# The first MLP's w_in by seven products for its last 1024 tokens, with the attention ahead of it ordered by batches

## The chip, the cores and the metric

The kernel runs on one core of one Trainium2 chip. The metric is device time in microseconds, the median over runs. A profiled execution gives a trace: what each engine did, when, and what ended each wait. TensorE is PE in its rows (its weight loads are PEld), VectorE is DVE, ScalarE is ACT, SyncE, which issues most loads, is SP.

## The reference

Linear attention with a norm, then two MLPs on its 4608 tokens:

```python
kv = np.einsum('bhsd,bhse->bhde', k, v)            # batch 8, heads 8, seq 576, head_dim 64
out = np.einsum('bhsd,bhde->bhse', q, kv)
rms = np.sqrt(np.mean(out * out, axis=-1, keepdims=True) + 1e-06)
x = (out / rms * g_norm).transpose(0, 2, 1, 3).reshape(4608, 512)
h = x @ moe_w_in                                   # 512 x 2048
x = (h * (1.0 / (1.0 + np.exp(-h)))) @ moe_w_out   # 2048 x 512
h = x @ moe2_w_in
r = np.maximum(h, 0.0)
return (s * (r * r) + b) @ moe2_w_out
```

## The kernel before

A product of two fp32 matrices is made of three fp32r matmul passes: each operand is split into a rounded high part and the rest (`xh` and `xl`, `wh` and `wl`; a "split" is a cast on ScalarE and a difference on VectorE), and high x high, high x low and low x high are summed in PSUM. A matmul takes a 128x128 weight tile and up to 512 tokens.

The kernel has four stages, one for each weight matrix. Stages 2 to 4 (`Output`, `Hidden`) use seven products: rows and columns are halved, and four half products by eight become seven products of sums of quarters (P1 to P7), the sums of the weights being made ahead and kept in DRAM (`wd`). Stage 1 is plain: nine blocks j of 512 tokens, each 16 groups m of 12 matmuls (`emit_h`, L469 to L501), whose PSUM tile `ph` ScalarE turns by Silu into g; g goes to DRAM (`gt`), from where stage 2 loads it.

The program's order is written by hand: one loop over (j, m) emits a group, then what `first_stage` (L926) puts behind it. Each engine runs its instructions in the order in which they are written. Beside block j stands the attention of tokens 512(j+1) to 512(j+2), four tiles t of 128 tokens, which may lie across two batches (`load_next` and `emit_next`, L544 to L572): keys times values at m = 2 (`emit_kv`, tile `pkv`), the transpose of q from m = 3 on (`emit_qT`, `pq`), q times kv at m = 4 to 7 (`out_tile`, `po`, whose squares go to a sum and whose copy goes to the page `xnp`), the root by some small VectorE steps, the scaling of `xnp` at m = 10 and 11, and the transposes of x at m = 11 to 14 (`xT_tile`, `px`), from which ScalarE makes `xh` and VectorE `xl` of the next block. The PSUM tiles `pkv`, `pq`, `po` and `px` take turns in two buffers (tag `a`), `ph` in two others.

`do_some(steps, n)` runs n steps of the weight preparation of stages 2 and 3: a step is one part of the decoding of raw weights (`rebias` on ScalarE, `low`, `sign`, `merge` on VectorE, L149), of their sums, or one split whose result goes to `wd`. `defer(1, f)` issues a store one group later. `room(tag, ...)` is a named place in SBUF, and who writes it waits for all who used it before.

Of the kernel before, what the change touches and what calls it, by code (L numbers as in the profile page):

```python
# [17 lines left out]
def kernel(  # L18
# [36 lines left out]
    nc = tc.nc  # L55
# [55 lines left out]
    def token_runs(t0, n):  # L111
        done = 0
        while done < n:
            b, s = divmod(t0 + done, S)
            step = min(n - done, S - s)
            yield done, step, b, s
            done += step

# [47 lines left out]
    hi_t = {}  # L166

    def decode_first(i, *steps):
        for step in steps:
            if step == "high":  # L170
                h = hi_t[i] = room(f"W{12 + 2 * i}", [P, WN], F32R, f"wh{i}")
                nc.scalar.copy(h, wf_t[1, i])
            elif step == "rest":
                l = room(f"W{13 + 2 * i}", [P, WN], F32R, f"wl{i}")
# [184 lines left out]
    def load_q(t):  # L359
        a = q_pages[t % TT // 2][:, t % 2].rearrange("p (h d) -> p h d", h=H)  # L360
        for off, n, b, s in token_runs(t * P, P):
            nc.sync.dma_start(a[off:off + n], q[b, :, s:s + n, :].rearrange("h p d -> p h d"))
        q_t[t] = a

    def emit_qT(t):
        a = q_t.pop(t).rearrange("p h d -> p (h d)")
        ps = ps_a.tile([P, T], F32, tag="a", name=f"pq{t}")
        for p in range(NP):
            nc.tensor.transpose(ps[:, p * P:(p + 1) * P], a[:, p * P:(p + 1) * P], ident)  # L369
        qT = at_kvw[:, 0].rearrange("p (a t) -> p a t", a=NP)  # L370
        nc.scalar.copy(qT.rearrange("p a t -> p (a t)"), ps)
        qT_t[t] = qT

    def emit_out(t, ps, pairs):

        po = ps.rearrange("p h d -> p (h d)")
        for p in pairs:
            for off, n, b, s in token_runs(t * P, P):
                nc.tensor.matmul(  # L379
                    po[off:off + n, p * P:(p + 1) * P], qT_t[t][:, p, off:off + n], kvw[b % 2][:, p, :],  # L380
                    start=True, stop=True,
                )

    def emit_squares(t, ps, ms):

        sq = work.tile([P, H, D], F32, tag="sg", name=f"sq{t}", bufs=3)
# [3 lines left out]
    def rsqrt_steps(r):  # L390

        ms, h, y, a = (r[:, i, :] for i in range(4))
# [21 lines left out]
    def xn_page(t):  # L414
        return xn_pages[t % TT // 2][:, t % 2].rearrange("p (h d) -> p h d", h=H)
# [9 lines left out]
    def out_tile(t):  # L425
        j, i = divmod(t, TT)
        if i == 0:
            r_t[j] = small.tile([P, 4, TT * H], F32, tag="r", name=f"r{j}", bufs=1)
        ps = ps_a.tile([P, H, D], F32, tag="a", name=f"po{t}")
        emit_out(t, ps, range(NP))  # L430
        emit_squares(t, ps, r_t[j][:, 0, i * H:(i + 1) * H])
# [3 lines left out]
    def norm_tile(t):  # L435
        j, i = divmod(t, TT)
        emit_norm(t, xn_t[t], r_t[j][:, 2, i * H:(i + 1) * H])
# [5 lines left out]

    def emit_xT(t, ps):
        xn = xn_t.pop(t).rearrange("p h d -> p (h d)")
        for p in range(NP):
            nc.tensor.transpose(ps[:, p, :], xn[:, p * P:(p + 1) * P], ident)  # L447
        j, i = divmod(t, TT)
        xh, xl = x_tiles(j)
        c = slice(i * P, (i + 1) * P)  # L450
        nc.scalar.activation(xh[:, :, c], ps, AF.Identity, scale=gcol)  # L451
        nc.vector.scalar_tensor_tensor(xl[:, :, c], ps, gcol, xh[:, :, c], op0=ALU.mult, op1=ALU.subtract)

    def xT_tile(t):
        emit_xT(t, ps_a.tile([P, NP, P], F32, tag="a", name=f"px{t}"))
# [13 lines left out]
    def emit_h(j, m):  # L469
# [8 lines left out]
        if j < NB - 2:  # L478

            i = m % 2  # L480
            if i == 0:
                g_t[0] = room(f"W{4 + m // 2 % NA}", [P, 2, T], F32, f"g{j}_{m}")
            both = g_t[0]
            g, rows = both[:, i], slice(m - 1, m + 1)
        else:
            i = 1
            tag = f"W{m}" if j == NB - 2 and m < 3 * NA else ("gh_0", "gh_1", "gl_0", "gl_1")[m % 4]
            g = room(tag, [P, T], F32, f"g{j}_{m}")
        nc.scalar.activation(g, ps, AF.Silu)  # L489
        run_late()  # L490
        if i == 0:
            return
        if j == 0:
            to = gt[1][0][rows].rearrange("i h p t -> p (i h) t")
            defer(1, lambda: nc.scalar.dma_start(to, both.rearrange("p i (h t) -> p (i h) t", h=2)))
        elif j < NB - 2:
            to = gt[1][(j + 1) // 2][rows, (j + 1) % 2].rearrange("i p t -> p i t")
            defer(1, lambda: nc.scalar.dma_start(to, both))
        else:
            to = gt[1][(j + 1) // 2][m, (j + 1) % 2]  # L500
            defer(1, lambda: nc.scalar.dma_start(to, g))  # L501
# [25 lines left out]
    def first_qT(t, qs):  # L527
# [10 lines left out]
        qT_t[t] = qT.rearrange("p (a t) -> p a t", a=NP)  # L538
# [3 lines left out]
    XT0 = 2 * TT + 3  # L542

    def load_next(j, m):  # L544

        t0 = TT * (j + 1)
        if m < TT:
            load_q(t0 + m)
        if 4 <= m < 4 + NP and j + 2 < B:
            load_kv(j + 2, m - 4)  # L550

    def emit_next(j, m):

        t0 = TT * (j + 1)
        if m == 2 and j + 1 < B:
            emit_kv(j + 1, range(NP))
        i = m - NP
        if 0 <= i < TT:
            out_tile(t0 + i)
        if -1 <= i < TT - 1:  # L560
            emit_qT(t0 + i + 1)
        if i == TT - 1:
            between.extend(rsqrt_steps(r_t[j + 1]))
        if j > 0 and 0 <= i - TT + 1 < 3:
            run_between(4)
        if m in (XT0 - 1, XT0):
            run_between(len(between))
            i = 2 * (m - XT0 + 1)
            norm_tile(t0 + i)
            norm_tile(t0 + i + 1)  # L570
        if XT0 <= m < XT0 + 4:
            xT_tile(t0 + m - XT0)  # L572

# [8 lines left out]
    class Hidden:  # L582
# [5 lines left out]
        def __init__(self, stage):  # L588
            self.grid, self.gt = grid[stage], gt[stage]
# [3 lines left out]

        def load(self, b, o):

            opening = b == order[0]
            tag = {self.B11: "Q", self.B12: "XA", self.B22: "XB", self.B21: "K" if opening else "Q"}[o]
            h, c = int(o in (self.B12, self.B22)), 2 * int(o in (self.B21, self.B22))
            x = self.raw[b, o] = pair(tag, f"xs{b}_{o}")[:, :, :size[b]]
            nc.sync.dma_start(x, yt[b][c:c + 2, h].rearrange("c p t -> p c t"))  # L600

        def combine(self, b, o):
# [5 lines left out]
            elif o == self.T2:  # L608
                to = pair("wf_0", f"xt2_{b}")[:, :, :size[b]] if b == order[0] else self.raw[b, self.T1]
# [6 lines left out]
        def split(self, b, k):  # L616
# [11 lines left out]
            self.slots[b, k] = [[t[:, c] for c in range(2)] for t in (hi, lo)]  # L628
            nc.scalar.copy(hi, src)
            nc.vector.tensor_sub(lo, src, hi)  # L630

        def before(self, k, a):

            b = order[0]
# [11 lines left out]
        def behind(self, b, i, k):  # L646

            nb = self.next_of.get(b)
            if i == 0 and b == order[0] and k in (P5, P6, P2):
# [21 lines left out]
        def product(self, g, k):  # L671
# [5 lines left out]
            a = self.grid.tiles[k, i // 2][:, i % 2].rearrange("p s (c f) -> p s c f", c=2)  # L677
            x = self.slots[b, k]
            for n, (s, t) in enumerate(PASSES):
                for c in range(2):  # L680
                    nc.tensor.matmul(  # L681
                        ps, a[:, s, c], x[t][c], start=(k in (P1, P5) and n == c == 0),
# [6 lines left out]
        def out(self, g, f, h, slots):  # L689
            b = self.seq[g][0]  # L690
            self.turn += 1
            r = room(self.G_ROOMS[self.turn % (4 if b else 7)], [P, T], F32, f"g{b}_{f}_{h}")[:, :size[b]]
# [3 lines left out]
        def square(self, g, f, h, ps):  # L696
            r = self.out(g, f, h, 2)
# [3 lines left out]
        def add_square(self, g, f, h, x, y):  # L701
# [5 lines left out]
            nc.vector.scalar_tensor_tensor(r, r, 0.0, r, op0=ALU.max, op1=ALU.mult)  # L707
# [32 lines left out]
    class Output:  # L740
# [96 lines left out]
        def rows_out(self, b, h, r):  # L837
# [6 lines left out]
            if b == 0:  # L844
                rows = out[:T].rearrange("(p c) d -> c p d", c=TT)[2 * h + r]
            else:
                rows = out[(2 * b - 1 + h) * T + r * P:][:P]
            defer(1, lambda: nc.scalar.dma_start(rows, o))
# [75 lines left out]
    out2, hidden3, out4 = Output(2), Hidden(3), Output(4)  # L924

    def first_stage(j, m, steps):  # L926

        if j + 1 < NB:
            load_next(j, m)
# [12 lines left out]
        if j + 1 < NB:  # L942
            emit_next(j, m)
        if j > 0:
            do_some(steps, 3 if m >= 12 else 2)
        elif m == MT - 1:
            do_some(steps, 1)
        if j == NB - 2 and m >= 4:
            grid[2].load()
        if j == NB - 1:  # L950
            if m < 4:
                out2.load(m + 1)
            else:
                out2.load(m - 7)
            if m >= 2:
                grid[2].load()
            if m in (10, 12):
                out2.make(m // 2 - 4)
# [33 lines left out]
    with tc.manual_schedule():  # L992
# [26 lines left out]
        r = r_t[0] = small.tile([P, 4, TT * H], F32, tag="r", name="r0", bufs=1)  # L1019
# [7 lines left out]
        for t in range(TT):  # L1027
            emit_out(t, pss[t], (0, 1))
# [3 lines left out]
        for p in (2, 3):  # L1032
            first_kv(p)
            for t in range(TT):
                emit_out(t, pss[t], (p,))
            load_kv(1, p)
        for t in range(TT):
            emit_squares(t, pss[t], r[:, 0, t * H:(t + 1) * H])
        decode_first(1, "high")
        warm_up(4)  # L1040
        for step in rsqrt_steps(r):
            step()
        for t in range(TT):
            emit_norm(t, pss[t], r[:, 2, t * H:(t + 1) * H])
        for t in range(TT):
            if t < 2:
                xT_tile(t)
            else:
                emit_xT(t, ps_y.tile([P, NP, P], F32, tag=f"y{t - 2}", name=f"px{t}"))
# [22 lines left out]
        for j in range(NB):  # L1072
# [3 lines left out]
        do_some(steps, 1000)  # L1076
# [37 lines left out]
```

## Time and profile before

| what | value |
|---|---|
| median of 3 runs | 1576.95 us (1576.92 to 1578.34) |
| the profiled execution | 1576.17 us |
| its span, from the first to the last instruction | 1574.4 us |
| TensorE busy | 1554.8 us, 99% of the span |
| VectorE, ScalarE busy | 959.1 us (61%), 802.7 us (51%) |
| mean DMA rate over the span | 222 GB/s |

Matmuls are pipelined and their ends are modelled, so the time of one matmul is read from start to start of a row and the next, not from its own duration. An engine's wait is named by what ended it. Durations in rows are in us unless marked ns.

### The profile page before, as it was taken

To read this page: it belongs to the slowest core of one execution; us is meant where nothing else is said; L and a number is where in the kernel's file an instruction comes from. 1 tells how busy PE (TensorE), PEld (TensorE's weight loads), DVE (VectorE), ACT (ScalarE), POOL (GpSimd) and SP (SyncE) were. 2 spreads that over 40 slices of the span, in tenths; PEclk is the share of its full clock that TensorE was granted. 3 is DMA by queue.
4 is the path that set the end of the run, shared out by engine and by line. 5 is a ranking of instruction groups with operands and counts; after the bars stand their busy time and mean duration, and the time that the engine had idled before them with its cause. 6 is when DMAs were issued, how large, how long until landed. Compare 5 with 4: busy or idle time off the path is not lost.

```text
span 1574.4 us, 21756 instructions
## 1 busy us (share of the span) xinstructions
PE 1554.8 (99%) x8232; PEld 1307.6 (83%) x8232; DVE 959.1 (61%) x1298; ACT 802.7 (51%) x1268; POOL 1.6 (0%) x8
## 2 busy tenths in 40 slices
PE   7999999999999999999999999999999999999998
PEld 5888888888888888888889788888889888888888
DVE  4736544654420958586857676767655858585745
ACT  3644554555432444444445565656555454555455
POOL 0000000000000000000000000000000000000000
PEclk9999999999999999999999999999999999999999
DMA  8978998796779663636259956574566982626251
GB/s 254 276 222 280 292 290 267 270 309 222 234 254 325 222 216 106 232 100 236 88 169 345 352 201 232 193 260 168 214 230 253 349 285 94 228 83 229 89 160 55
DMA packets 225609, 349.58 MB, mean 222 GB/s; under 512 B 56544, under 2 KB 94432, under 8 KB 225504
## 3 DMA queue, kind: packets, MB, share of 16 engines
q1 hardware_dynamic: 160064, 238.85, 46.3%
q10 hardware_dynamic: 65440, 109.34, 18.6%
q8 instruction: 65, 1.06, 0.3%
q14 instruction: 40, 0.33, 0.1%
HBM read 209.72 MB, written 138.41 MB: 221 GB/s over the span
## 4 chain that ended last, share of the span: by engine, by line
PE 93%; DMA 4%; DVE 1%; ACT 1%; issue 0%; SPq 0%; ACTq 0%; DVEq 0%
PE ph L475 25%; PE qy L891 18%; PE qv L891 12%; PE qx L891 12%; PE py L681 9%; PE px L681 6%; PE pv L681 6%; PE po L379 2%; PE px L447 1%; DMA r<-gt 1%; PE pkv L349 1%; PE pq L369 1%; PE pt L841 1%; DMA wd<-wp 1%; DMA kvz<-in_v_dram 1%; DMA kv<-in_v_dram 1%
## 5 line engine op out<-in xcount | busy, mean ns | idle before, releaser
L891 PE MATMUL qy<-o,w 128*128 128x512 f32 (+1 forms) x1440 | 299.2, 368 | 0.1
L891 PEld LDWEIGHTS qy<-o,w 128*128 128x128 f32 x1440 | 251.1, 188 | 45.2 <-DVE o L814 0.3
L814 DVE TENSOR_TENSOR o<-ka,o 128x1024 fp32r<-128x1024 f32 (+1 forms) x160 | 178.5, 1116 | 155.5 <-ACT o L812 154.8
L812 ACT CAST o<-ka 128x1024 fp32r<-128x1024 f32 (+1 forms) x160 | 153.8, 965 | 154.9 <-PE qv L891 69.3
L891 PE MATMUL qv<-o,w 128*128 128x512 f32 (+1 forms) x960 | 203.2, 369 | 1.4 <-DVE o L814 1.2
L891 PE MATMUL qx<-o,w 128*128 128x512 f32 (+1 forms) x960 | 202.7, 369 | 0.0
L489 ACT ACTIVATE g<-ph 128x512 f32<-128x512 f32 x144 | 86.2, 599 | 219.3 <-PE ph L475 214.6
L891 PEld LDWEIGHTS qv<-o,w 128*128 128x128 f32 x960 | 167.0, 189 | 31.2 <-DVE o L814 1.8
L891 PEld LDWEIGHTS qx<-o,w 128*128 128x128 f32 x960 | 167.1, 189 | 29.6
L681 PE MATMUL py<-x,w 128*128 128x512 f32 (+1 forms) x720 | 162.1, 369 | 1.8 <-ACT g L704 1.4
L475 PE MATMUL ph<-xh,wh 128*128 128x512 f32 x576 | 162.7, 404 | 0.8 <-ACT xh L451 0.8
L475 PE MATMUL ph<-xl,wh 128*128 128x512 f32 x576 | 154.8, 390 | 0.0
L475 PE MATMUL ph<-xh,wl 128*128 128x512 f32 x576 | 154.7, 390 | 0.0
L681 PEld LDWEIGHTS py<-x,w 128*128 128x128 f32 x720 | 126.2, 188 | 26.3 <-ACT g L704 2.0
L475 PEld LDWEIGHTS ph<-xl,wh 128*128 128x128 f32 x576 | 108.1, 188 | 23.9
L475 PEld LDWEIGHTS ph<-xh,wl 128*128 128x128 f32 x576 | 108.1, 188 | 23.5
L812 ACT CAST o<-r 128x1024 fp32r<-128x1024 f32 (+1 forms) x80 | 77.1, 964 | 87.6 <-PE qy L891 40.2
L475 PEld LDWEIGHTS ph<-xh,wh 128*128 128x128 f32 x576 | 102.2, 188 | 18.8 <-ACT xh L451 1.2
L681 PE MATMUL pv<-x,w 128*128 128x512 f32 (+1 forms) x480 | 111.6, 368 | 0.0
L681 PE MATMUL px<-x,w 128*128 128x512 f32 (+1 forms) x480 | 111.6, 368 | 0.0
L814 DVE TENSOR_TENSOR o<-r,o 128x1024 fp32r<-128x1024 f32 (+1 forms) x80 | 89.4, 1118 | 33.4 <-ACT o L812 33.2
L681 PEld LDWEIGHTS px<-x,w 128*128 128x128 f32 x480 | 84.8, 189 | 15.1
(114 smaller groups left out, 1620.6 us busy)
## 6 DMA issues: line engine op xcount, KB each, us to landing
r<-gt SPq DMA_DIRECT2D x96, 512.0 KB, 5.1
w<-wd SPq DMA_DIRECT2D x84, 512.0 KB, 6.7
gt<-g ACTq DMA_DIRECT2D x160, 256.0 KB, 2.5
gt<-g ACTq DMA_DIRECT2D x56, 512.0 KB, 4.8
wd<-wo SPq DMA_DIRECT2D x112, 256.0 KB, 4.0
wr<-in_moe_w_in_dram SPq DMA_DIRECT2D x16, 1024.0 KB, 6.5
wr<-in_moe_w_out_dram SPq DMA_DIRECT2D x16, 1024.0 KB, 6.1
ka<-gt SPq DMA_DIRECT2D x32, 512.0 KB, 4.0
```

The source lines that it names most:

```text
L349: nc.tensor.matmul(ps[r, p, r], ka[:, i, d], va[:, i, d], start=(p == pairs[0] and c == 0), stop=False, skip_group_check=True,)
L369: nc.tensor.transpose(ps[:, p * P:(p + 1) * P], a[:, p * P:(p + 1) * P], ident)
L379: nc.tensor.matmul(po[off:off + n, p * P:(p + 1) * P], qT_t[t][:, p, off:off + n], kvw[b % 2][:, p, :], start=True, stop=True,)
L447: nc.tensor.transpose(ps[:, p, :], xn[:, p * P:(p + 1) * P], ident)
L475: nc.tensor.matmul(ps, wt[:, c, :], xt[:, c, :], start=(n == 0 and c == 0), stop=(n == 2 and c == KT - 1))
L489: nc.scalar.activation(g, ps, AF.Silu)
L681: nc.tensor.matmul(ps, a[:, s, c], x[t][c], start=(k in (P1, P5) and n == c == 0), stop=(n == 2 and c == 1), skip_group_check=True,)
L812: nc.scalar.copy(o[:, :, 0], x)
L814: nc.vector.tensor_sub(o[:, :, 1], x, o[:, :, 0])
L841: nc.tensor.transpose(ps[:, e * P:(e + 1) * P], self.c[b, h, e][:, r * P:(r + 1) * P], ident)
L891: nc.tensor.matmul(ps, t[:, s], self.o[u][:, i, p], start=(k in (P1, P5) and a == i == m == 0), stop=(a == NA - 1 and i == 1 and m == 2), ...
```

## The change

Stage 1 now has seven plain blocks (`PB = 7`) and, for the last 1024 tokens, the class `Hidden` that stage 3 has (`Hidden(1, order1)`): eight pairs of 128 columns, and for each seven products of six matmuls. Tokens are taken in another order. A batch b has 576 tokens: four tiles of 128 and a tail of 64. Block 0 is batch 0's first 512 tokens, blocks 1 to 6 those of the batches 1, 2, 4, 5, 6 and 7 (`FROM`). The 1024 left are batch 3's first 512 and the eight tails, two tails to a tile. Their x, one fp32 tile after another, is evicted by ScalarE alone into one of two rooms and stored to DRAM (`xt`), and loaded again in block 6. The last stage writes its rows to the places that this order means (`rows_of`).

The attention is ordered by batches: `attend(slot)`, with slot = 16 j + m, and `UNITS` with (batch, tiles, first slot). For a unit at slot s the keys and values are multiplied at s - 2, q is transposed from s - 1, q times kv stands at s to s + n - 1, and the transposes of x at s + n + 3 to s + 2n + 2.

The sums of w_in for the seven products are made in SBUF from the split weights (`combine_first`), by one generator of 56 steps (`combos`), 14 of them in block 6 and the rest beside the products. The products of the quarters a11, a12 and a22 use the split weights as they are. Loads of stage 2's weights (`grid[2].load`), which stood in the last two plain blocks, now stand in the new stage (six of them) and in the first block of stage 2.

```diff
+    PB = 7
+    FROM = {1: 1, 2: 2, 3: 4, 4: 5, 5: 6, 6: 7}
+    BY_SEVEN = {(4, 0): 3}
+    order1 = [4]
...
     def emit_xT(t, ps):
+        b, i = t
         xn = xn_t.pop(t).rearrange("p h d -> p (h d)")
         for p in range(NP):
             nc.tensor.transpose(ps[:, p, :], xn[:, p * P:(p + 1) * P], ident)
...
+        if i < TT and b in BLOCK:
+            xh, xl = x_tiles(BLOCK[b])
+            c = slice(i * P, (i + 1) * P)
+            nc.scalar.activation(xh[:, :, c], ps, AF.Identity, scale=gcol)
+            nc.vector.scalar_tensor_tensor(xl[:, :, c], ps, gcol, xh[:, :, c], op0=ALU.mult, op1=ALU.subtract)
+            return
+        to = xt[order1[-1]][1, b // 2] if i == TT else xt[SEVEN[b][0]][SEVEN[b][1], i]
+        staged[0] += 1
+        x = room(("gh_1", "gl_1")[staged[0] % 2], [P, KT, P], F32, f"xs{b}_{i}")
+        nc.scalar.activation(x, ps, AF.Identity, scale=gcol)
+        defer(1, lambda: nc.scalar.dma_start(to, x))
...
+    UNITS = [(1, 5, 4), (2, 4, 18), (3, 5, 27), (4, 4, 36), (5, 5, 52), (6, 4, 68), (7, 5, 84)]
+
+    def attend(slot):
+
+        for b, n, s in UNITS:
+            d = slot - s
+            lead = 4 if b == 1 else 6
+            if 0 <= d + lead < n:
+                load_q(b, d + lead)
+            if 0 <= d < NP and b + 1 < B:
+                load_kv(b + 1, d)
+        for b, n, s in UNITS:
+            d = slot - s
+            if d == -2:
+                emit_kv(b, range(NP))
+            if 0 <= d < n:
+                out_tile((b, d))
+            if -1 <= d < n - 1:
+                emit_qT((b, d + 1))
+            if d == n - 1:
+                between.extend(rsqrt_steps(r_t[b], n))
...
+            if n + 3 <= d < 2 * n + 3:
+                xT_tile((b, d - n - 3))
...
+    def combine_first(i):
...
+        if i < 2:
+            fs = [room(tag, [P, KT, P], F32, f"cf{i}_{tag}") for tag in ("gh_0", "gh_1")]
...
+        def part(n):
+            k, src = ((P5, s5), (P6, s6), (P7, s7), (P3, s3))[n]
+            h, l = place(n)
+            first_w[k, i] = [[x[:, c] for c in range(2)] for x in (h, l)]
+            nc.scalar.copy(h, src)
+            nc.vector.tensor_sub(l, src, h)
+
+        yield lambda: whole(1)
+        yield lambda: whole(0)
+        yield lambda: nc.vector.tensor_add(s5, a21, a22)
+        yield lambda: (nc.vector.tensor_sub(s6, s5, a11), part(0))
+        yield lambda: (nc.vector.tensor_sub(s7, a11, a21), part(1))
+        yield lambda: (nc.vector.tensor_sub(s3, a12, s6), part(2))
+        yield lambda: part(3)
...
+    def first_of_seven(m):
+
+        x, b = hidden1, order1[0]
+        if m == 1:
+            for o in (x.B11, x.B12, x.B22, x.B21):
+                x.load(b, o)
+        if m < 14:
+            do_some(combos, 1)
...
+        if m == 15:
+            x.split(b, P2)
+            x.split(b, P7)
+
+    def beside1(b, i, k):
+        if (i, k) > (0, P6) and not (i == 0 and k not in (P2, P7)):
+            do_some(combos, 2 if k in (P1, P6) else 1)
+        if i >= 2 and k == P5:
             grid[2].load()
...
-        for j in range(NB):
+        for j in range(PB):
             for m in range(MT):
                 emit_h(j, m)
                 first_stage(j, m, steps)
-        do_some(steps, 1000)
+        hidden1.run(beside1)
```

What the change moves is seen in the order of the instructions on an engine. On TensorE, at the end of block 5 before (`px27` is the last transpose for block 6, `ph6_0` block 6's first group):

```order
L447 MATMUL px27_3430<-ident_63,xnp1_71 128x128 x4
L475 MATMUL ph5_15_3442<-xh5_2830,wh7_788 128x512 x4
L475 MATMUL ph5_15_3442<-xl5_2831,wh7_788 128x512 x4
L475 MATMUL ph5_15_3442<-xh5_2830,wl7_813 128x512 x4
L475 MATMUL ph6_0_3467<-xh6_3342,wh0_229 128x512 x4
L475 MATMUL ph6_0_3467<-xl6_3343,wh0_229 128x512 x4
```

and of the change at the same place (`px7_2` and `px7_3` are tiles 2 and 3 of batch 7):

```order
L461 MATMUL px7_2_3724<-ident_63,xnp1_71 128x128 x4
L495 MATMUL ph5_15_3736<-xh5_3107,wh7_806 128x512 x4
L495 MATMUL ph5_15_3736<-xl5_3108,wh7_806 128x512 x4
L495 MATMUL ph5_15_3736<-xh5_3107,wl7_826 128x512 x4
L461 MATMUL px7_3_3751<-ident_63,xnp1_71 128x128 x4
L495 MATMUL ph6_0_3767<-xh6_3667,wh0_230 128x512 x4
L495 MATMUL ph6_0_3767<-xl6_3668,wh0_230 128x512 x4
```

The last transposes stood one group ahead of the block that reads their x, and now stand right ahead of its first matmul. It is the same at the ends of blocks 0 and 3; at those of blocks 1, 2 and 4 there are three, one and one groups between.

On TensorE, in block 1 of the change, groups 11 and 12 (slots 27 and 28; `px2` transposes x of batch 2, `po3` and `pq3` are batch 3's; before, `px` stood alone at these places):

```order
L495 MATMUL ph1_11_1392<-xh1_863,wl5_710 128x512 x4
L461 MATMUL px2_2_1413<-ident_63,xnp1_71 128x128 x4
L385 MATMUL po3_0_1421<-kvw1_72,at_kvw_67 128x128 x4
L375 MATMUL pq3_1_1430<-ident_63,qp0_68 128x128 x4
L495 MATMUL ph1_12_1441<-xh1_863,wh6_749 128x512 x4
L495 MATMUL ph1_12_1441<-xl1_864,wh6_749 128x512 x4
L495 MATMUL ph1_12_1441<-xh1_863,wl6_781 128x512 x4
L461 MATMUL px2_3_1460<-ident_63,xnp1_71 128x128 x4
L385 MATMUL po3_1_1467<-kvw1_72,at_kvw_67 128x128 x4
L375 MATMUL pq3_2_1476<-ident_63,qp1_69 128x128 x4
```

Three tiles of the two `a` buffers now follow each other between two groups; before there were at most two.

On ScalarE, from the last plain group of the change into the new stage (`x4_3` and `x4_4` are the high parts of the splits for P2 and P7, `px0` and `py0` the accumulators of the first pair of columns):

```order
L502 ACTIVATE g6_14_4117<-ph6_15_4120 128x512
L656 CAST x4_3_4134<-x1_4_2_3829 128x4x2x128
L656 CAST x4_4_4137<-x1_4_1_3825 128x4x2x128
L753 COPY py0_4147<-px0_4140 128x512
L512 DMA gt1_3_163<-g6_14_4117 128x2x512
L758 COPY u0_4164<-py0_4147 128x512
```

Two casts stand between the last Silu and the copy of `py0`, to which the third product on TensorE, P6, adds.

## Rows read from the trace of the kernel before

**Rows 1.** The page's sections 1 and 4: busy time, chain that ended last.

```profile
PE 1554.8 (99%) x8232; PEld 1307.6 (83%) x8232; DVE 959.1 (61%) x1298; ACT 802.7 (51%) x1268; POOL 1.6 (0%) x8
...
PE 93%; DMA 4%; DVE 1%; ACT 1%; issue 0%; SPq 0%; ACTq 0%; DVEq 0%
```

**Rows 2.** Waits of TensorE, 37 to 1215 us: total us, times, longest.

```profile
PE py L681 <- ACT g L704: 1.4, 2, 0.9
PE qv L891 <- DVE o L814: 1.2, 1, 1.2
PE ph L475 <- ACT xh L451: 0.8, 1, 0.8
PE py L681 <- ACT u L725: 0.3, 1, 0.3
```

**Rows 3.** Windows: length; PE, PEld, DVE, ACT, POOL; clock; DMA share; GB/s.

```profile
105.70:375.80 270.10, 270.10 (x1699) 226.29 (x1698) 143.78 (x306) 138.67 (x280) 0.00 (x0) 1.00 0.86 283
...
815.30:896.00 80.70, 79.20 (x504) 71.50 (x502) 56.75 (x83) 42.43 (x73) 0.00 (x0) 1.00 0.92 340
906.00:1160.00 254.00, 253.99 (x1121) 209.96 (x1120) 170.24 (x255) 153.35 (x265) 0.00 (x0) 1.00 0.58 210
```

**Rows 4.** The chain in order of time, 464 to 530 us: start, length.

```profile
464.34 46.29 PE ph L475 x204
```

**Rows 5.** Timeline of TensorE in stage 3: start, length, engine, line.

```profile
890.27 1.52 PE L681 MATMUL px<-x,w 128*128 128x512 f32 x6
891.63 1.52 PE L681 MATMUL py<-x,w 128*128 128x512 f32 x6
```

**Rows 6.** Timeline of TensorE, block 1, groups with two attention tiles.

```profile
108.74 1.05 PE L379 MATMUL po<-kvw,at_kvw 128*128 128x128 f32 x8
109.63 0.60 PE L369 MATMUL pq<-ident,qp 128*128 128x128 f32 x4
109.99 1.17 PE L475 MATMUL ph<-xh,wh 128*128 128x512 f32 x4
```

**Rows 7.** Timeline of TensorE, block 1, groups with one transpose of x.

```profile
132.80 0.60 PE L447 MATMUL px<-ident,xnp 128*128 128x128 f32 x4
133.16 1.18 PE L475 MATMUL ph<-xh,wh 128*128 128x512 f32 x4
...
136.02 0.60 PE L447 MATMUL px<-ident,xnp 128*128 128x128 f32 x4
...
142.46 0.60 PE L447 MATMUL px<-ident,xnp 128*128 128x128 f32 x4
```

**Rows 8.** Timeline of ScalarE at the same place (ACTq: its issue of a store).

```profile
133.00 0.60 ACT L489 ACTIVATE g<-ph 128x512 f32<-128x512 f32 x1 [1.49 <-PE ph L475]
133.49 0.68 ACT L451 ACTIVATE xh<-px,gcol 128x512 fp32r<-128x512 f32 x1
...
136.28 0.37 ACTq L498 DMA_DIRECT2D gt<-g  x1
```

**Rows 9.** Timeline of VectorE at the same place.

```profile
134.21 0.75 DVE L452 SCALAR_TENSOR_TENSOR xl<-px,gcol,xh 128x512 fp32r<-128x512 f32 x1 [0.77 <-ACT xh L451]
...
142.90 1.23 DVE L160 SCALAR_TENSOR_TENSOR wf<-wr 128x1024 int32<-128x1024 int32 x1
144.05 0.74 DVE L452 SCALAR_TENSOR_TENSOR xl<-px,gcol,xh 128x512 fp32r<-128x512 f32 x1
```

**Rows 10.** DMAs issued from 105 to 376 us: count, size, median us to landing.

```profile
wd<-wo SPq DMA_DIRECT2D x95, 256.0 KB, 4.4
gt<-g ACTq DMA_DIRECT2D x40, 512.0 KB, 4.8
```

**Rows 11.** Timeline of ScalarE at the opening of stage 4.

```profile
1206.88 2.00 ACT L812 CAST o<-ka 128x1024 fp32r<-128x1024 f32 x2 [0.52 <-DVE o L814]
```

**Rows 12.** Groups of VectorE, 906 to 1160 us: count, busy us, mean ns, idle before.

```profile
L236 DVE TENSOR_TENSOR wp<-ws,wp 128x256 fp32r<-128x256 f32 x28 | 11.9, 424 | 32.8 <-ACT wp L235 32.8
L226 DVE TENSOR_TENSOR csum<-csum,wf 128x512 f32<-128x512 f32 x14 | 9.6, 688 | 0.2
```

More of the change, by code (lines that the diff above doesn't have):

```diff
@@ L442, in x_tiles @@
         return x_t[j]
+    BLOCK = {0: 0, **{b: j for j, b in FROM.items()}}
+    SEVEN = {b: place for place, b in BY_SEVEN.items()}
+    xt = {b: dram.tile([2, TT, P, KT, P], F32, name=f"xt{b}") for b in order1}
+    staged = [0]
     def emit_xT(t, ps):
+        b, i = t
         xn = xn_t.pop(t).rearrange("p h d -> p (h d)")
@@ L477, in emit_h @@
                 )
[L478 to L489, printed above, removed]
+        i = m % 2
+        if i == 0:
+            g_t[0] = room(f"W{(4 if j < PB - 1 else 8) + m // 2 % NA}", [P, 2, T], F32, f"g{j}_{m}")
+        both = g_t[0]
+        nc.scalar.activation(both[:, i], ps, AF.Silu)
         run_late()
@@ L492, in emit_h @@
             return
+        rows = slice(m - 1, m + 1)
         if j == 0:
@@ L632, in before @@
         def before(self, k, a):
-            b = order[0]
+            b = self.order[0]
             if (k, a) == (P7, 0):
@@ L648, in behind @@
             nb = self.next_of.get(b)
-            if i == 0 and b == order[0] and k in (P5, P6, P2):
+            if i == 0 and b == self.order[0] and k in (P5, P6, P2):
                 if k == P5:
@@ L676, in product @@
             ps = self.of(kind, g)
-            a = self.grid.tiles[k, i // 2][:, i % 2].rearrange("p s (c f) -> p s c f", c=2)
+            a = self.weights(k, i)
             x = self.slots[b, k]
@@ L691, in out @@
             self.turn += 1
-            r = room(self.G_ROOMS[self.turn % (4 if b else 7)], [P, T], F32, f"g{b}_{f}_{h}")[:, :size[b]]
+            r = room(self.G_ROOMS[self.turn % (4 if b and self.stage == 3 else 7)], [P, T], F32, f"g{self.stage}_{b}_{f}_{h}")[:, :size[b]]
             defer(slots if b else slots + 1, lambda: nc.scalar.dma_start(self.gt[b][f, h], r))
@@ L696, in square @@
         def square(self, g, f, h, ps):
+            if self.stage == 1:
+                nc.scalar.activation(self.out(g, f, h, 2), ps, AF.Silu)
+                return
             r = self.out(g, f, h, 2)
@@ L844, in rows_out, with store @@
             if b == 0:
-                rows = out[:T].rearrange("(p c) d -> c p d", c=TT)[2 * h + r]
-            else:
-                rows = out[(2 * b - 1 + h) * T + r * P:][:P]
-            defer(1, lambda: nc.scalar.dma_start(rows, o))
+                t = (0, 2 * h + r)
+            elif b not in order1:
+                t = (FROM[2 * b - 1 + h], r)
+            else:
+                t = (BY_SEVEN[b, h], r) if (b, h) in BY_SEVEN else (2 * r + 1, TT)
+            def store():
+                for part, rows in rows_of(*t):
+                    nc.scalar.dma_start(rows, o[part])
+            defer(1, store)
         def end_of(self, b, k):
@@ L926, in first_stage @@
+    combos = (f for i in range(NF) for f in combine_first(i))
     def first_stage(j, m, steps):
-        if j + 1 < NB:
-            load_next(j, m)
         if j == 0:
@@ L941, in first_stage @@
                     decode_first(i + 3, "sign", "merge")
[L942 to L948, printed above, removed]
-            grid[2].load()
[L950 to L958, printed above, removed]
+        attend(MT * j + m)
+        if j == 0:
+            if m == 10:
+                do_some(steps, 1)
+            elif m > 12:
+                do_some(steps, 2)
+        elif j == 1:
+            do_some(steps, 2 if m < 12 else 1)
+        elif j < PB - 1:
+            do_some(steps, 2 if m < 8 else 3)
+        else:
+            if m < 12:
+                do_some(steps, 2)
+            elif m == 12:
+                do_some(steps, 1000)
+            first_of_seven(m)
+    def first_of_seven(m):
[5 more added lines that the diff above has]
+            do_some(combos, 1)
+        if m == 7:
+            x.combine(b, x.T1)
+        if m == 8:
+            x.split(b, P1)
+        if m == 9:
+            x.combine(b, x.T2)
+        if m == 10:
+            x.split(b, P5)
+            x.combine(b, x.B12)
+        if m == 13:
+            x.split(b, P6)
+        if m == 15:
[5 more added lines that the diff above has]
+        if i >= 2 and k == P5:
+            grid[2].load()
+        if i == 3 and k == P1:
+            out2.load(2)
+        if i == NF - 1:
+            if k == P6:
+                out2.load(4)
+            if k in (P1, P7):
+                out2.make({P1: 1, P7: 2}[k])
     def beside2(b, k, a):
```

188 lines of the change are left out of this document (107 added, 81 removed).

## Prediction

> **The bound.** I read the page's head first: one core, TensorE busy 99% of the span and 93% of the chain that ended last [rows 1]. The reader should then look at what TensorE waited for between 37 and 1215 us [rows 2]: four kinds of wait, 3.7 us in all, one of them (ph <- xh) at the first hand-over from attention to matmuls and the others in the second and third stage. So TensorE is the bound in every stage, it has no slack to give, and a stall anywhere in the first MLP is paid in full. The windows [rows 3] say the same by stage: from 105.7 to 375.8 us (five blocks with attention) TensorE is busy 270.10 of 270.10 us, VectorE 143.78, ScalarE 138.67 (just over half), the DMA engines 0.86 of the time at 283 GB/s, and the granted clock is 1.00, the upper level (2.4 GHz). So the change is worth the TensorE time that it removes, less every place where TensorE is now made to wait.
>
> **Removed.** One 512-token block of w_in is 16 groups of 12 matmuls. Two plain blocks are 384; seven products are 8 pairs x 7 x 6 = 336. A plain matmul costs 46.29 us / 204 = 0.227 us [rows 4], and six of a product take 891.63 - 890.27 = 1.36 us, 0.227 each [rows 5]. So 48 x 0.227 = -10.9 us. The Silu, the stores of g and the attention matmuls are the same in number.
>
> **Moved.** Call slot s the group m of block j with s = 16j + m. Attention now comes in seven units at the slots of UNITS. Where no two meet, a unit of n tiles puts its work in 2n+2 slots: 4 x 12 + 3 x 10 = 78, against 79 before (nine slots of each block, and ten where keys and values are multiplied). Ten of the 78 meet in pairs, so there are 68 places where TensorE leaves the fp32r matmuls for attention, 11 fewer. Leaving and coming back has a price of its own: behind px the 12 matmuls take 136.02 - 133.16 = 2.86 us [rows 7] where 12 x 0.227 = 2.72 us is the plain price, 0.14 us. Two pieces in one slot pay it once, if one goes over into the other for nothing, as pq behind po seems to (0.36 us there and in a slot of its own kind, px [rows 6, 7]). So 11 x 0 to 0.14; I take -1.0 us, nearer the upper end.
>
> **Hand-overs.** Before, the last px of a block stood in group 14, one group ahead of the block that reads it. Units 1, 5 and 7 have five tiles, and their tile 3 is transposed at slots 15, 63 and 95, right ahead of blocks 1, 4 and 6. What TensorE then waits for can be laid out from one slot of before: the transposes start at 132.80 [rows 7]; on ScalarE comes the Silu at 133.00, behind it the xh eviction at 133.49 for 0.68 us [rows 8], so xh is there at 134.17, about 1.42 us behind the start with the hop to TensorE; the transposes need only 0.36. The stall is 1.05 us. The second operand, xl, is needed four matmuls (0.9 us) later. VectorE starts it 0.04 us behind xh and takes 0.75 [rows 9], so it is in time if VectorE is free. At slot 95 it stands behind `sign` and `merge`; the same row order stood in group 14 of a block before, where merge ran from 142.90 and xl from 144.05, 1.59 us behind its transposes at 142.46 instead of 1.41 [rows 7, 9]: still just in time. Bounds: 0 if ScalarE were free at once (not possible behind the Silu), 2.2 if xl is late by another merge (1.2). 3 x 1.05 = +3.15 us.
>
> **PSUM buffers.** All attention tiles of TensorE share two buffers (`a`). At slots 27 and 28 px of batch 2, po and pq of batch 3 follow each other, so pq waits until xh and xl have left px's buffer. From rows 7 to 9: xl ends 134.21 + 0.75 = 134.96, 2.16 us behind the start of px; pq would start at 0.36 + 0.89 = 1.25 (po's length [rows 6]). That is 0.95 us, twice: +1.9 us. At slots 36 to 38 the px is of batch 3, whose x goes to DRAM by one ScalarE eviction and no xl: 1.42 - 1.25 = 0.17 us, three times, +0.5 us.
>
> **Staging rooms.** The five evictions at slots 35 to 39 use two rooms in turn. A store is issued a slot later, 0.26 us behind the end of its matmuls (136.28 against 136.02), and the room is wanted 5.0 us after that (a slot of 4.6 us and the 0.69 us to the eviction, less 0.26). In these blocks a 256 KB transfer takes 4.4 us to land, a 512 KB one 4.8 [rows 10]: by the median no wait, for slow ones one of a us or so. Ends: 0, and 3.6 us (three rooms at 1.2 late); I take +0.5. The Trainium skill, "DMA: Bandwidth & Descriptors", section "Anatomy of one DMA", fits about 2.0 us plus bytes / 436 GB/s (on the GpSimd path), which would be 2.6 us for 256 KB, an estimate; by it this term is zero and the sum 0.5 us lower, but the row here has 4.4 us.
>
> **The opening.** At the end of block 6 ScalarE has the Silu, two casts of 128x1024 (a pair takes 2.00 us [rows 11]) and only then the copy of py that the third product adds to. Silu issued at 0.20, casts from 0.69 to 2.65, copy (0.5) to 3.15; two products take 2.72. +0.45 us. The opening of the third stage had such a wait of 0.9 us (the longer of py <- g [rows 2]); that is the upper end, 0 the lower.
>
> **At nothing.** (a) The weight sums, eight pairs of columns: per pair two adds of 128x512 at 0.69, four sums and four differences of 128x256 at 0.42 on VectorE [rows 12], 4.8 us. Two pairs are made in block 6 (VectorE 33 us of 44 there). The others come nine steps a pair of columns where seven make one: 6.1 us, and with two output adds of 0.69 VectorE has 7.5 us of work in the 9.5 us of a pair. TensorE covers it; every accumulator is wanted back two products (2.7 us) later at the earliest. (b) VectorE's first weight sum, at block 6 group 0, writes the room (gh_1) from which the last staged tile is still to be stored; that store is issued a slot later and lands some 4.4 us after, so VectorE stands for about 6 us. Behind it are weight splits, whose data the first product wants 14 slots later. Without that cover it would be 6 us. (c) 22 of the 28 w_out tiles now load in the second stage's first block instead of the last plain blocks, five units of 2.7 us ahead of their use; the last stage loads its own in this way and its opening shows no wait in rows 2. (d) Bytes: blocks 1 to 5 ask for about 16.2 MB each, counted from the DMAs in the code (g 4.2, q, k and v 3.8, staged x 0.4, weights 7.8). They take 43.6 us of plain matmuls and 6/5 of a batch, which costs 270.1 / 5 - 43.6 = 10.4; that is 56 us and 289 GB/s, against the 283 of rows 3.
>
> **The sum.** -10.9 - 1.0 + 3.15 + 1.9 + 0.5 + 0.5 + 0.45 = -5.4 us. The profiled execution took 1576.17 us (span 1574.4 and 1.8 around it), 0.8 below the median of 1576.95; so 1570.8 for such an execution and 1571.5 on the scale of the medians, 0.35% faster. A difference of 0.2% (3.2 us: 1573.8 to 1580.1) is about what a measurement of this kernel can tell from none.
>
> **Rivals.** *B, nothing waits*: the evictions turn out to lie beside TensorE after all. It is 1576.95 - 10.9 - 1.5 = 1564.5 us. For it: TensorE's waits in rows 2 are few. Against it: the same eviction chain cost 0.8 us the one time that it had no slack (ph <- xh [rows 2]). *C, the gain is eaten*: the DMA engines are late where batches crowd. At slots 34 to 39 about 8.4 MB are asked in 27 us (six slots of 2.72 and one batch's products and tiles), 307 GB/s; at the 283 of rows 3 they take 29.7, 2.4 us late, and late keys or rooms stop TensorE; with hand-overs at twice my price (xl late too) it is 1571.5 + 2.4 + 3.15 = 1577. For it: 0.86 busy leaves little. Against it: from 815.3 to 896 us the same engines moved 340 GB/s [rows 3]. *D, slower*: VectorE becomes the bound of the new stage. If each of its split halves waits for ScalarE's half (about 1 us, five a pair), 7.5 becomes 12.5 us a pair against 9.5, and five pairs lose 3 us each: 1571.5 + 15 = 1586.5. It decides from about 11.3 us a pair (a loss of 8.6 over five, back past 1580.1). Against it: in the hidden stage of the second MLP VectorE ran 170.24 of 254.00 us with such splits between, and TensorE never stopped [rows 3].
>
> **Chances.** The forecast 0.54 (its own range 1568.5 to 1574), B 0.10, C 0.25, D 0.11. Faster by over 0.2%: forecast and B, 0.64; within: C, 0.25; slower: D, 0.11. For eight in ten the range takes the forecast, C and half of B: 1566 to 1579.
>
> **Signs.** In the profile after: the plain matmuls at 1344 and a new group of 336 products; ph waiting for the xh eviction three times, about 1 us each, at the starts of blocks 1, 4 and 6; pq waiting twice for xl and three times, less, for the staged eviction; one wait of the new py for ScalarE. VectorE idle for about 6 us early in block 6, by a store. The prediction is wrong if TensorE waits inside the new stage, if kv or q from DRAM appear among TensorE's releasers in blocks 1 and 2, or if none of the hand-over waits is there.

## The result and the profile after

The changed kernel took 1597.17 us (median of 4 runs, 1590.43 to 1598.5) beside 1576.93 for the kernel before: 1.012 times as long, 95% interval 1.009 to 1.015. The forecast was 1571.5, with 1566 to 1579 for eight in ten; it was wrong by 26 us and in its sign. The profiled execution took 1598.04 us (span 1595.9), 21.9 us more than that of before.

The page's head and chain, which answer to [rows 1]:

```profile
PE 1561.9 (98%) x8184; PEld 1305.3 (82%) x8184; DVE 1007.3 (63%) x1385; ACT 833.1 (52%) x1331; POOL 1.6 (0%) x8
...
PE 88%; DMA 6%; ACT 2%; DVE 2%; issue 1%; ACTq 1%; SPq 0%; DVEq 0%
```

TensorE has 48 instructions fewer and is busy 7.1 us longer. So fewer matmuls are done, and something makes them dearer, beside the waits: DMA has grown from 4 to 6% of the chain. The waits of TensorE from 37 to 1219 us, which answer to [rows 2] (in all, times, longest):

```profile
PE py L708 <- ACT g L734: 5.0, 4, 2.6
PE ph L495 <- ACT xh L465: 3.3, 4, 0.8
PE pq L375 <- ACT xs L471: 1.9, 2, 1.4
PE qx L931 <- ACT o L845: 1.7, 1, 1.7
PE pq L375 <- DVE xl L466: 1.5, 2, 0.8
PE qv L931 <- DVE o L847: 1.0, 1, 1.0
PE qx L931 <- DVE o L847: 0.8, 1, 0.8
```

The second, third and fifth were forecast. The fourth, the sixth and the seventh, and most of the first, stand in later stages, whose matmuls and their order are unchanged; the sixth was there before, with 1.2 us [rows 2]. One more lies in the last stage, from 1219 us on:

```profile
PE qv L931 <- ACT o L845: 2.9, 1, 2.9
```

To see where the time went I took, from one profile of each kernel, the time of each stage from its first matmul to the first of the next (the last stage: to its last matmul). It has the experiments too:

| kernel | plain blocks | new stage | stage 2 | stage 3 | stage 4 |
|---|---|---|---|---|---|
| before | 473.6 | | 346.8 | 348.8 | 363.4 |
| changed | 395.7 | 78.6 | 351.8 | 355.9 | 372.0 |
| changed, second profile (e12) | 397.3 | 78.7 | 354.8 | 351.5 | 371.5 |
| e1, room r of 768 bytes | 397.6 | 77.9 | 351.7 | 348.9 | 368.3 |
| e5, e1 with two edits in stages 2 and 4 | 396.7 | 78.0 | 347.4 | 350.3 | 365.4 |
| e6, e1 with edits in the plain blocks | 387.0 | 77.9 | 351.4 | 347.8 | 368.6 |
| e7, all of these edits | 386.5 | 78.0 | 347.5 | 350.3 | 364.9 |
| e9, as e7 with room r as in the change | 386.7 | 78.6 | 349.6 | 351.2 | 366.5 |

Stage 1 (the first two columns) is 0.7 us longer than before where the sum had 5.4 less. The other 20.7 us were lost in stages 2 to 4, for which the sum had no term at all. A first cause shows in the chain of stage 2 in order of time (start, length), in rows of 48 equal matmuls. Before:

```profile
510.63 10.88 PE qx L891 x48
521.51 10.88 PE qv L891 x48
532.39 10.88 PE qy L891 x48
```

and after (the first `qx` of the stage, ahead of these rows, has the waits of its opening):

```profile
525.36 11.09 PE qv L931 x48
536.46 11.15 PE qy L931 x48
547.61 10.88 PE qx L931 x48
```

Two of the seven products (P5 and P6) are slower with nothing waiting and the granted clock at 1.00, its upper level, and the same two in each of the four batches whose products have 512 columns.

### The profile page after: what moved, and what is told of

Same layout as the page of the kernel before. It is cut to its first block, busy times and chain, and to the rows that moved or that the text cites. A ratio compares the mean times of both kernels' runs of the same rounds, so it can differ in the third digit from the quotient of the medians.

```text
span 1595.9 us, 21844 instructions
## 1 busy us (share of the span) xinstructions
PE 1561.9 (98%) x8184; PEld 1305.3 (82%) x8184; DVE 1007.3 (63%) x1385; ACT 833.1 (52%) x1331; POOL 1.6 (0%) x8
## 4 chain that ended last, share of the span: by engine, by line
PE 88%; DMA 6%; ACT 2%; DVE 2%; issue 1%; ACTq 1%; SPq 0%; DVEq 0%
PE ph L495 19%; PE qy L931 18%; PE qv L931 11%; PE py L708 11%; PE qx L931 11%; PE px L708 7%; PE pv L708 7%; PE po L385 2%; DMA gt<-g 1%; PE pkv L351 1%; PE pq L375 1%; DMA r<-gt 1%; PE px L461 1%; PE pt L874 1%; DMA out_dram<-out 1%
## 5 line engine op out<-in xcount | busy, mean ns | idle before, releaser
L931 PE MATMUL qv<-o,w 128*128 128x512 f32 (+1 forms) x960 | 207.6, 374 | 4.1 <-ACT o L845 2.9
L502 ACT ACTIVATE g<-ph 128x512 f32<-128x512 f32 x112 | 67.0, 598 | 154.4 <-PE ph L495 152.0
L495 PE MATMUL ph<-xh,wh 128*128 128x512 f32 x448 | 128.1, 408 | 3.3 <-ACT xh L465 3.3
L495 PE MATMUL ph<-xl,wh 128*128 128x512 f32 x448 | 121.3, 393 | 0.0
L495 PE MATMUL ph<-xh,wl 128*128 128x512 f32 x448 | 120.2, 390 | 0.0
L495 PEld LDWEIGHTS ph<-xl,wh 128*128 128x128 f32 x448 | 84.6, 189 | 19.1 <-DVE xl L466 0.2
L495 PEld LDWEIGHTS ph<-xh,wl 128*128 128x128 f32 x448 | 84.4, 188 | 18.3
L708 PEld LDWEIGHTS pv<-x,w 128*128 128x128 f32 x480 | 85.2, 190 | 16.0
```

The source lines that it names most:

```text
L495: nc.tensor.matmul(ps, wt[:, c, :], xt[:, c, :], start=(n == 0 and c == 0), stop=(n == 2 and c == KT - 1))
L502: nc.scalar.activation(both[:, i], ps, AF.Silu)
L708: nc.tensor.matmul(ps, a[s][c], x[t][c], start=(k in (P1, P5) and n == c == 0), stop=(n == 2 and c == 1), skip_group_check=True,)
L931: nc.tensor.matmul(ps, t[:, s], self.o[u][:, i, p], start=(k in (P1, P5) and a == i == m == 0), stop=(a == NA - 1 and i == 1 and m == 2), ...
```

## The experiments

They were measured at different times, at which the kernel before took 1576.55 to 1578.31 us, so a difference between two of them holds to some 2 us; the ratios are to the kernel before at the same time.

**Addresses.** Two things differ for stage 2: its weights are loaded beside its first batch, and its operands lie elsewhere. As the same products are slow in later batches as well, where none of these loads is left, it may be the addresses. The tile `r` (the sums of squares) grew from 512 to 640 bytes a partition, since a unit can have five tiles, and every room allocated behind it moved by 128 bytes, while those ahead of it stayed: among them seven of the weight rooms. In the program as compiled (the traces hold no addresses), before, all fp32r matmuls have both operands at the same address modulo 256; after, 1464 of 6720 have them 128 apart, in stage 2 all of P6 and 36 of 48 matmuls of P5 among them. Theory A: that is the price. Rival B: transfers are late. Four kernels, each with one line changed:

```diff
e1, in the changed kernel
-            r_t[b] = small.tile([P, 4, (TT + 1) * H], F32, tag="r", name=f"r{b}", bufs=1)
+            r_t[b] = small.tile([P, 4, (TT + 2) * H], F32, tag="r", name=f"r{b}", bufs=1)
e2, in the kernel before
-            r_t[j] = small.tile([P, 4, TT * H], F32, tag="r", name=f"r{j}", bufs=1)
+            r_t[j] = small.tile([P, 4, (TT + 1) * H], F32, tag="r", name=f"r{j}", bufs=1)[:, :, :TT * H]
e3, in the kernel before, ahead of its first tile
+    pad = room("pad", [P, 32], F32, "pad")
e4: as e2, with 576 bytes
```

> The changed kernel with its tile r of 768 bytes a partition instead of 640 (before: 512), so that every room allocated behind r lies 256 bytes further on than before, not 128. Nothing is computed otherwise. Theory A (addresses): a fp32r matmul whose moving operand and weights lie at SBUF addresses that differ modulo 256 takes 231.5 ns instead of 226.7; the change made 1464 of 6720 such, here none: six of a product back to 1.36 us everywhere, 7 us off the sum at least, and up to 20 if the stalls of stages 2 to 4 come with it: 1577 to 1590 us. Rival B (transfers): the later stages lose by late transfers and the half-clock stretches behind them, whatever the addresses: 1594 to 1598 us, with the P5 and P6 products still at 1.39.

Measured: 1588.14 us, 9.0 less than the changed kernel, 1.0066 of the kernel before (1.0054 to 1.0078). The products are at 10.88 again, in the chain of stage 2 (start, length):

```profile
528.42 10.88 PE qv L931 x48
539.30 10.88 PE qy L931 x48
```

> The kernel before with nothing but its tile r made 640 bytes a partition instead of 512 (what is behind it is never used). By the addresses 1380 of 6768 fp32r matmuls then have operands 128 bytes apart modulo 256, the same products as in the changed kernel. Theory A: those take 231.5 ns, 6.6 us in all, and the time is 1583 us or more (to 1595 if stalls follow). Rival B: 1577 us, products at 1.36 us throughout.

Measured: 1582.8 us against 1578.31, ratio 1.003 (1.002 to 1.004), 4.5 us more where theory A counted 6.6; and the chain of its stage 2 has the slow products of the changed kernel, though everything is computed and ordered as before:

```profile
519.47 11.09 PE qv L891 x48
530.56 11.16 PE qy L891 x48
541.72 10.88 PE qx L891 x48
```

> The kernel before with an unused room of 128 bytes a partition ahead of everything: all operands move by 128 bytes together and none differ. If it is the difference of the two operands' addresses that counts (theory A): 1577 us, every product at 1.36 us. If it is the position itself that is slow (modulo 256 equal to 160): slower than the kernel before in all 6768 matmuls, up to 32 us.

Measured: ratio 0.9996 (0.9987 to 1.0005), 10.88 for each 48 in stages 2 and 4.

> The kernel before with the tile r of 576 bytes a partition: the same 1380 matmuls have operands 64 bytes apart instead of 128. Theory A with a step of 256: slower as with 640 bytes, by about 6.6 us (1583). If only a difference of 128 matters, or addresses are compared modulo 64: 1577.

Measured: 1580.95 us, ratio 1.0022 (1.0013 to 1.0031); 10.96 and 10.99 for the two products, so 64 bytes cost less than 128, which theory A had not foreseen. Moving both operands together does nothing, the distance between them does: in this theory A holds. By the products of the changed kernel's profile the price is 1.9 us in stage 2, 3.4 in stage 3 (four batches whose eight pairs take 0.89 more than eight of 9.52, less 0.2 in the half batch), 1.9 in stage 4 and 0.7 in the new stage: 7.9 us. It is not all: e1 is still 0.66% slower than before. Whether rival B holds for that part, these four runs do not tell.

**What is left in stages 2 and 4.** In e1 the second stage's opening still has two gaps. The chain there (start, length; ACTq is ScalarE's issue of a store):

```profile
510.81 7.78 DMA gt<-g
...
518.66 0.33 ACTq L720
...
519.03 1.05 ACT o L845
...
520.11 1.23 DVE o L847
521.38 3.62 PE qx L931 x8
```

A store of g issued at 510.81 lands 7.8 us later, while the DMA engines move 376 GB/s (243 in the 7.8 us before). ScalarE's queue stands ahead of its last such store until then: eight completion counters serve all the transfers of SyncE and ScalarE, and that store has the counter of the one issued at 510.81. The cast of the second stage's third operand is written behind it on ScalarE. The Trainium skill, "PSUM — Partial Sum Buffer", section "Engine vs sequencer instructions", says that ScalarE's queue is strictly first in, first out; this chain agrees, the cast starting 0.04 us behind the end of that issue.

Near 1550 us, the chain in the changed kernel:

```profile
1544.58 0.60 ACTq L886
...
1545.23 0.61 ACTq L886
...
1545.87 4.08 DMA out_dram<-out
...
1550.61 0.61 ACTq L886
1551.22 0.04 issue
1551.26 0.61 ACTq L886
```

Here the four output tiles that hold two tails each are stored, in two parts each. Before, every one of the 36 output tiles went out whole; after, `rows_of` splits these four, and all four stand together, since the tails are one half of batch 4 in the new order, right ahead of the last, short batch. An issue holds ScalarE's queue for 0.5 to 0.6 us, an eviction waits for its room until a store has landed 4.08 us after its issue, and the casts for the next product stand behind.

```diff
e5, in the kernel of e1
+            if self.stage == 1 and g == len(self.seq) - 1:
+                slots += 6
             defer(slots if b else slots + 1, lambda: nc.scalar.dma_start(self.gt[b][f, h], r))
...
-                for part, rows in rows_of(*t):
-                    nc.scalar.dma_start(rows, o[part])
+                for i, (part, rows) in enumerate(rows_of(*t)):
+                    (nc.scalar, nc.sync)[i].dma_start(rows, o[part])
```

> The kernel of e1 (room r of 768 bytes), and two places in later stages: the four stores of the last pair of columns of the new seven-product stage are issued six slots later, behind the casts of the second stage's first operands; and where a tile of output rows goes out in two parts (the four tiles that straddle two batches), the second part is issued by SyncE and not by ScalarE. Theory A: the second stage's opening loses 2.8 us because a store stands ahead of the casts on ScalarE until an earlier store with the same completion counter has landed (7.8 us after its issue), and the last stage loses 3.0 us near 1546 us because eight issues of 0.6 us stand ahead of a cast; both go, with their half-clock stretches (1.7 each): 1579 to 1583 us, the second stage 347 to 348 us from its first matmul to the third's, the fourth 364 to 365. Rival B: the operands are late because the transfers that bring them are late, whoever issues what: both stages as in e1 (351.7 and 368.3), 1588 us.

Measured: 1580.27 us, ratio 1.0014 (1.0001 to 1.0026), 7.9 us less than e1; stage 2 is 4.3 us shorter and stage 4 2.9. The gap at the opening is gone, with the loads of the second stage where they were:

```profile
511.18 1.36 PE pv L708 x6
512.54 10.88 PE qx L933 x48
```

Near 1546 us TensorE had waited 3.0 us in e1; here it is 0.3. The first edit acts in stage 2 alone and the second in stage 4. Who issues the stores, and when, was the cause; rival B is out for both places.

**The first stage.** The waits that the prediction had listed in the plain blocks can be taken away without moving a matmul of w_in:

```diff
e6, in the kernel of e1
-    UNITS = [(1, 5, 4), (2, 4, 18), (3, 5, 27), (4, 4, 36), (5, 5, 52), (6, 4, 68), (7, 5, 84)]
+    UNITS = [(1, 5, 3), (2, 4, 18), (3, 5, 27), (4, 4, 36), (5, 5, 51), (6, 4, 68), (7, 5, 83)]
...
-        ps = ps_a.tile([P, T], F32, tag="a", name=f"pq{t[0]}_{t[1]}")
+        bank_turn["q"] ^= 1
+        ps = bank(f"y{bank_turn['q']}_0", f"pq{t[0]}_{t[1]}")
...
+            bank_turn["x"] ^= 1
+            ps = psum.tile([P, NP, P], F32, tag=f"y{2 + bank_turn['x']}_0", name=f"px{t[0]}_{t[1]}")
...
-        defer(1, lambda: nc.scalar.dma_start(to, x))
+        nc.scalar.dma_start(to, x)
...
+        attend(-1)
         for j in range(PB):
```

> The kernel of e1, and in the plain blocks: the units of batches 1, 5 and 7 begin one slot earlier (no transposes right ahead of blocks 1, 4 and 6); the transposes of q and of x have two PSUM buffers each of their own (the four that stand idle until the new stage); the staged x is stored at once and not a slot later. Theory A: all waits that the prediction listed go, 3 x 1.05 for the hand-overs, 1.9 and 0.8 for PSUM, 1.5 for the staging room, 7.4 us: the stage from its first matmul to the second stage's 468 us, the time 1581 us. Rival: the earlier units bring q or kv later than they are wanted, and 1 to 3 us come back as waits on DMA: 1583 us.

Measured: 1576.69 us, ratio 0.9997 (0.9988 to 1.0006): 11.5 us less than e1, more than the 7.4 expected. The plain blocks are 10.6 us shorter. The staging room had cost e1 more than the changed kernel's first profile shows: slot 38 was 3.3 us and slot 39 1.5 us too long in e1, the second with the granted clock at 0.50 from 193.6 us on. Of the rival one wait came: the second q tile, 0.8 us.

> The edits of e5 and e6 together. If the terms add: 1588 - 7 - 7 = 1574 us, 0.3% below the kernel before; if they don't (each wait removed shows the next): 1578 to 1582.

Measured: 1568.28 us, ratio 0.9939 (0.9925 to 0.9954). The terms add: 7.9 and 11.5 less make 1568.7. This is the version that beats both kernels, by 9 us the one before. The waits of TensorE that are left in it from 37 to 1219 us:

```profile
PE py L716 <- ACT g L744: 3.1, 3, 2.0
PE qv L941 <- DVE o L857: 1.8, 1, 1.8
PE ph L503 <- ACT xh L468: 0.8, 1, 0.8
PE py L716 <- ACT py L763: 0.5, 2, 0.3
PE pq L378 <- DMA qp<-in_q_dram: 0.5, 1, 0.5
```

**The addresses again, with the waits gone.** The tile r of e7 at 640 bytes:

> The kernel of e7 with the tile r of 640 bytes again, as in the change. Theory A (the addresses have a price of their own, whatever waits): 1464 fp32r matmuls slow again, 8 us by the products of the changed kernel's profile: 1576.5 us. Rival (in the changed kernel the addresses only cost by the waits that they set off, which the other edits took away): 1568 to 1571.

Measured: 1575.02 us, ratio 0.9989 (0.998 to 0.9998), 6.7 us above e7, and P6 of stage 2 is slow again in its chain:

```profile
523.90 11.16 PE qy L941 x48
```

The rival falls: the address difference has its own price, near the 7.9 counted.

**Other distances**, from single products of one profile each:

> The kernel before with the tile r 32 bytes a partition longer: 1380 fp32r matmuls have operands 32 bytes apart modulo 256 instead of none (64 in e4, 128 in e2). Read from single products in the profile: if the extra time of a matmul grows with the distance (0 at none, some 2 ns at 64, 5 at 128), about 1 ns here, 48 of them in 10.93 us; if any distance costs alike, 10.96 to 10.99 as with 64.

> The kernel before with r 96 bytes longer, for single products only: 48 matmuls of 512 columns in 11.1 to 11.2 us, if only differences of a multiple of 256 are free; 10.88 if 96 happens to be free.

> The kernel before with r 192 bytes longer: as with 64 (10.96 to 10.99), if the distance counts either way round; 11.1 to 11.2 if it grows with the distance up to 256.

Measured, 48 matmuls in us (of P5 36 have operands apart, of P6 all; "half" are the 256 columns of the last batch, P6):

| bytes apart | P5 | P6 | P6, half |
|---|---|---|---|
| 0 (before, e3) and 256 (e1) | 10.88 | 10.88 | 5.76 |
| 32 (e8) | 11.12 | 11.19 | 5.61 |
| 64 (e4) | 10.96 | 10.99 | 5.44 |
| 96 (e10) | 11.17 | 11.20 | 5.75 |
| 128 (e2) | 11.09 | 11.16 | 5.69 |
| 192 (e11) | 11.15 | 11.20 | 5.66 |

All distances tried but 256 cost the wide matmuls 2 to 8 ns each (at 96 and 192 P2, whose operands are not apart, took 10.92 and 10.91). What was expected at 96 came; that the price grows with the distance, that any distance costs as 64 does, or that 192 is as 64, was wrong. The whole times of e8, e10 and e11, one run each, were 1583.26, 1586.39 and 1584.94 us.

**By chance or not.**

> The changed kernel once more, for a second profile. In the first, two stalls near 1177 and 1186 us at the end of the third stage cost 4.9 us; the kernels of e1 and e9 have next to none there. If they belong to the change, the third stage takes 355 to 356 us again; if they come by chance with late stores, 351 to 353 (348.8 and 3.4 for the addresses), and the time lies at the lower end of 1590 to 1598. The second stage's opening and the stall near 1550 us, which have causes in the program, should be there again (351 to 352 and 371 to 372 us).

Measured: 1596.99 us, ratio 1.0123 (1.0105 to 1.014), where the lower end of 1590 to 1598 was expected. Stage 3 took 351.5 us: the two stalls near 1177 and 1186 us, 4.9 us with the half clock behind them, were not there. Stages 2 and 4 lost as before, stage 2 more (a stretch of 6.8 us with the granted clock at 0.50 from 520.6), and slot 38 was 3.4 us too long. So the stalls in stage 3 were seen in one of two profiles of the same kernel, and nothing shows that they belong to the change; what made the stores late there stays open.

## Why the prediction was wrong

The step that failed is the sum itself: it was made over stage 1 only. Stages 2 to 4 had no term in it, and they lost 20.7 us: by the operands' addresses (7.2) and the two-part stores (5.6), which the prediction did not see, by the second stage's opening (2.8), which it had looked at under (c) and held to be free, and by stalls in stage 3 in that profile (4.9). Inside stage 1 most terms were right and one was mis-sized. Point by point:

- **Removed and moved, -11.9: right.** In e7 the plain blocks and the new stage take 464.4 us against 473.6, 9.2 less, with 0.7 of wait for q, 0.8 at the new stage's opening and 1.0 at its end in it: without these 11.7. Only the two terms together are measured.
- **Hand-overs, +3.15: right.** The groups at slots 15, 63 and 95 took 4.26 us each where 3.20 is usual: 3.2. e6 takes them away.
- **PSUM buffers: right at slots 27 and 28,** 0.95 and 1.03 us longer than in e6 (forecast 0.95 each). Of the two that wait for the staged eviction alone, slot 36 was 0.7 longer and slot 37 0.2 (forecast 0.17 each).
- **Staging rooms, +0.5: mis-sized.** A store took 6.48 us where the median of the row is 4.4 [rows 10], and slot 38 was 1.6 too long in the first profile, 3.4 in the second, with a stretch behind it in which the granted clock was 0.50. The estimate of 2.6 us from the Trainium skill, "DMA: Bandwidth & Descriptors", section "Anatomy of one DMA", a fit for transfers that GpSimd issues while these are ScalarE's, is further off: the trace does not agree with it in this stretch, where the DMA engines were 0.86 busy before [rows 3]. The chain of the changed kernel there:

```profile
185.55 6.48 DMA xt<-xs
...
192.12 0.70 ACT xs L471
192.81 0.04 issue
192.86 0.66 PE pq L375 x4
```

- **The opening, +0.45:** 0.8 (products of 1.86, 1.49 and 2.88 us for 1.36, 1.36 and 2.72). The 1.0 us at the new stage's end, py behind ScalarE's copy of the last group, was not in the sum; a wait inside the new stage is one of the prediction's own signs of being wrong.
- **At nothing: (a) and (b) right, (c) wrong in what it left out.** VectorE was busy 42.46 of 77.20 us in the new stage and its pairs took 9.52 in e1, so rival D is out; and VectorE stood 6.0 us for the store, with no wait of TensorE behind it. The window of the new stage, its columns as in [rows 3], and VectorE's wait:

```profile
434.00:511.20 77.20, 76.19 (x331) 61.75 (x330) 42.46 (x82) 44.27 (x85) 0.00 (x0) 1.00 0.49 180
```

```profile
DVE cf_gh L992 <- DMA xt<-xs: 6.0, 1, 6.0
```

The 22 loads of w_out were held harmless by the example of the last stage. But that stage follows a half batch, whose stores are of 128 KB; here four of 256 KB and their counters stood among the loads. That the smaller stores are what spares the last stage is not tested. What e5 shows is that the loads alone cost the opening nothing: with the stores behind the casts the 2.8 us are gone.
- **Not in the sum:** the operands' addresses, 7.9 us (e1, e2 and e9), 0.7 of them in the new stage; the two-part stores that `rows_of` makes, 5.6 us at one product of stage 4 in the first profile (11.74 us for 6.15), half of it by the clock; the stalls of stage 3, 4.9; and in the first profile a stretch of 6.8 us at the start of block 0 with the granted clock at 0.50, where the kernel before had 3.4: 1.7 us, which the second profile does not have. Two windows of the changed kernel, its columns the same:

```profile
33.90:40.70 6.80, 6.02 (x21) 4.70 (x19) 6.58 (x9) 3.58 (x5) 0.00 (x0) 0.50 0.32 101
...
1552.80:1559.60 6.80, 6.23 (x27) 5.94 (x28) 6.11 (x10) 3.61 (x8) 0.00 (x0) 0.50 0.13 29
```

In each of the two the granted clock is 0.50, the lower level of 1.2 GHz. The second begins at 1552.8 us, in a wait of TensorE from 1550.3 to 1553.2 us.

For stage 1 the terms as measured, -11.7, 3.2, 2.0, 0.9, 1.6, 0.8, 1.0, 0.7 and 1.7, make 0.2 where the first profile has 0.7. For stages 2 to 4: 7.2 by the addresses there, 2.8, 5.6 and 4.9 make 20.5 where 20.7 were lost (by stages it is 0.3 and 1.0 more in 2 and 4 and 1.2 less in 3, of smaller waits). None of the rivals named a mechanism outside stage 1, so the range was too narrow as well. One part of rival C came, the room that is late at slots 34 to 39 (1.6 and 3.4 us where it had 2.4); its other part, hand-overs at twice the price, did not, and its 1577 us was far from what was measured.

## What to carry to other kernels

A change that resizes one tile moves every room behind it: compare the compiled addresses of the operands that meet in matmuls before and after, and pad the tile until their distances are what they were. Cost the stages that a change does not touch as well: follow what the stage ahead now leaves on ScalarE's queue (stores, and whose completion they wait for), and where its outputs are written. And when a change saves TensorE time but brings its own waits, price the waits one by one: here those in the plain blocks could be taken away with idle PSUM buffers, units one slot earlier and a store issued at once, and with the stores of the later stages moved as well 9 of the 11.9 us came out.

## What was not expected of the hardware

A fp32r matmul of 512 columns took 226.7 ns where its two operands lie a multiple of 256 bytes apart and 229 to 235 where they lie 32 to 192 bytes off; with 256 columns it was the other way round, 120 ns in the one case and 113 to 120 in the other, shortest at 64 bytes. Both operands 128 bytes further on together changed nothing. Why it is so, no run here tells.
